# Streamed weight halves: three transfers of 640 columns in place of two of 960

## The chip, the cores and the metric

The kernel runs on one core of one Trainium2 chip. The metric is the device time of one execution in microseconds; the median of several runs is compared. A profiled execution, taken by the hardware profiler, gives the trace that the views below are read from.

## The reference

Four layers are applied in turn to x (2,048 positions of 640 columns), each as `x = x + layer(layernorm(x))`: layer A, layer B, layer A, layer B, with the same weights for both A and both B.

```python
# A: a recurrence over 64 segments of 32 positions, with 8 memory rows
for s in range(n_seg):
    h = concat([mem, xs])                  # 40 rows of 640
    q, k, v = h @ Wq, h @ Wk, h @ Wv       # 32 heads of 192 each
    p = softmax(mask(q @ k.T * scale))
    o = (p @ v) @ Wo
    mem, out = o[:8], o[8:]                # the memory of the next segment
# B: sliding dilated attention, window 8, dilation 2, 32 heads of 20
q, k, v = x @ wqkv
o = attention(q, k[pos - 2*w], v[pos - 2*w], w = 0..7) @ wo
```

Everything is bf16. The memory rows make the segments of layer A a strict sequence, so its weights (Wq, Wk, Wv, Wo, each 640 x 6,144) are needed again for every segment.

## The kernel before

**Steps.** `run` makes 67 steps (t = 0 to 66), written out in full. In step t, layer 1 works on segment t and layer 3 on segment t - 2, side by side as two lanes of 40 rows (80 columns of every matmul). Layers 2 and 4 (B) follow one step behind. The step's matmuls on TensorE are laid down in a fixed order by hand (`manual_schedule`): for each of eight groups of four heads ("quads", i = 0 to 7) the projections k, q, v (`proj`, matmuls at L264), the scores, the values, and with a lag of five quads the output projection (`a_o`, matmuls at L381). The matmuls of B are put between them. VectorE, ScalarE and GpSimd empty PSUM, take exponentials and normalise beside this.

**Weights.** Each quad of each of the four weights is cut into two halves. A half is a tile of 128 partitions by `HALF` = 1,920 bf16 columns (3,840 bytes in a partition, 480 KB). There are 64 halves. SBUF holds 41 of them for the whole run (`wres`); the other 23 are *streamed*: they are loaded anew in every step into a ring of four tiles (`wring`, all with the name w_ring), spread evenly over the step's TensorE work (`resident_halves`). For k, q and v the half's columns are five chunks of the contraction, 384 columns each, and the first matmuls go through all five chunks; for o they are three blocks of 640.

**Loads.** All weight loads are issued by SyncE's queue, in the order in which TensorE consumes the halves. `prefetch` is called by `used` whenever a half has been read for the last time, which frees a slot of the ring:

```python
t_ = self.wring.tile([P, HALF], BF16, name="w_ring")
self.ring_free -= 1
kind, i, h = key
piece = HALF if self.n_loaded < N_HALVES else PIECE
self.n_loaded += 1
for c0 in range(0, HALF, piece):
    self.nc.sync.dma_start(out=t_[:, c0:c0 + piece], in_=self.wsrc[kind][i, h, :, c0:c0 + piece])
```

The loads of the first pass, all 64 halves, are one transfer of 480 KB each. From then on a streamed half is loaded in pieces of `PIECE` columns. The line that issues them is L226. A load into a ring slot waits on SyncE until TensorE's last matmul on the slot's former half is done, and SyncE's queue is in order: what stands behind a waiting load waits too. The weight loads of TensorE wait for the piece that holds their columns, not for the whole half. B's weights are loaded once, in the second pass. ScalarE's queue carries the input segments and the results.

Of the kernel before, what the change touches and what calls it, by code (L numbers as in the profile page):

```python
# [38 lines left out]
BDIL = 2  # L39

HALF = 1920
PIECE = 960
N_HALVES = 64
N_RES = 41
RING = 4
# [33 lines left out]
class Kernel:  # L79
# [130 lines left out]
    def prefetch(self):  # L210

        while self.loads and (self.loads[0] in self.resident or self.loads[0][0] == "b" or self.ring_free):
# [9 lines left out]
# [3 lines that stand above are left out]
# [693 lines left out]
```

## Time and profile before

| | |
|---|---|
| runs | 3134.16, 3138.03, 3148.04 us; median 3138.03 |
| the profiled execution | 3135.55 us, of which the span is 3133.8 |
| granted TensorE clock, mean | 0.992 |
| busy: PE, DVE, ACT, POOL | 98%, 76%, 59%, 18% |
| DMA, mean over the span | 251 GB/s |
| transfers of streamed halves in pieces | 2,990 of 240 KB |
| median us from issue to landing of these | 3.8 to 4.1, by weight |

PE is TensorE, PEld its weight loads, DVE is VectorE, ACT is ScalarE, POOL is GpSimd, SP is SyncE and SPq its queue of instructions. Busy time leaves out the issuing of transfers. In the chain of waits that ended last, 95% of the span lies on PE. The names in a row read "out<-in"; L264 is line 264 of the kernel. "Landing" is the moment at which a transfer's completion has arrived from all of its DMA engines.

### The profile page before, as it was taken

To read this page: it belongs to the slowest core of one execution; us is meant where nothing else is said; L and a number is where in the kernel's file an instruction comes from. 1 tells how busy PE (TensorE), PEld (TensorE's weight loads), DVE (VectorE), ACT (ScalarE), POOL (GpSimd) and SP (SyncE) were. 2 spreads that over 40 slices of the span, in tenths; PEclk is the share of its full clock that TensorE was granted. 3 is DMA by queue.
4 is the path that set the end of the run, shared out by engine and by line. 5 is a ranking of instruction groups with operands and counts; after the bars stand their busy time and mean duration, and the time that the engine had idled before them with its cause. 6 is when DMAs were issued, how large, how long until landed. Compare 5 with 4: busy or idle time off the path is not lost.

```text
span 3133.8 us, 187134 instructions
## 1 busy us (share of the span) xinstructions
PE 3080.9 (98%) x83420; PEld 3031.6 (97%) x83420; DVE 2375.7 (76%) x6019; ACT 1851.2 (59%) x5613; POOL 555.5 (18%) x1012
## 2 busy tenths in 40 slices
PE   6899999999999999999999999999999999999998
PEld 4899999999999999999999999999999999999997
DVE  3677777777777777777777777777777777777776
ACT  2456656656656656656656656655655655655654
POOL 2112111111111111111111111111111121121121
PEclk7999999999999999999999999999999999999999
DMA  9877777877778778777877877777778878777776
GB/s 390 294 251 248 246 247 246 249 246 249 246 245 249 248 246 250 246 246 247 250 244 250 248 244 249 249 246 246 248 244 248 249 245 249 248 244 244 249 248 215
DMA packets 455705, 786.98 MB, mean 251 GB/s; under 512 B 58864, under 2 KB 445680, under 8 KB 454896
## 3 DMA queue, kind: packets, MB, share of 16 engines
q1 hardware_dynamic: 441216, 769.80, 77.7%
q8 instruction: 652, 10.68, 1.4%
q10 hardware_dynamic: 13680, 5.21, 0.7%
q14 instruction: 157, 1.29, 0.1%
HBM read 772.19 MB, written 2.62 MB: 247 GB/s over the span
## 4 chain that ended last, share of the span: by engine, by line
PE 95%; DMA 3%; DVE 1%; ACT 0%; issue 0%; SPq 0%; ACTq 0%; DVEq 0%
PE ps_acc L381 18%; PE ps_k L264 17%; PE ps_q L264 17%; PE ps_v L264 17%; PE ps_vt L318 5%; PE ps_o L351 5%; PE ps_s L330 2%; PE ps_s L331 2%; PE ps_bs L538 2%; PE ps_bv L495 2%; PE ps_by L594 2%; PE ps_bk L495 1%; PE ps_bq L495 1%; DMA w_q<-in_A_Wq_dram 1%; PE ps_vr L298 1%; PE ps_bo L561 1%
## 5 line engine op out<-in xcount | busy, mean ns | idle before, releaser
L355 ACT ACTIVATE R<-ps_o 64x160 f32<-64x160 f32 (+1 forms) x2112 | 622.2, 295 | 336.6 <-PE ps_o L351 120.0
L264 PEld LDWEIGHTS <-w_ring 128*128 128x128 bf16 x16530 | 679.2, 100 | 20.9 <-issue 4.5
L526 POOL TENSOR_TENSOR QX<-QB,hmask 128x448 bf16<-128x448 bf16 (+1 forms) x325 | 311.3, 966 | 1339.5 <-ACT QB L505 1029.6
L264 PE MATMUL ps_q<-hT,w_q 128*128 128x80 bf16 (+1 forms) x12870 | 540.8, 201 | 3.4 <-DMA w_q<-in_A_Wq_dram 3.4
L264 PEld LDWEIGHTS <-w_q 128*128 128x128 bf16 x12870 | 493.5, 100 | 4.5 <-DMA w_q<-in_A_Wq_dram 4.4
L381 PE MATMUL ps_acc<-OT,w_o 128*128 128x80 bf16 (+1 forms) x9900 | 458.5, 201 | 2.7 <-DMA w_o<-in_A_Wo_dram 2.1
L276 ACT CAST KF<-ps_k 128x320 bf16<-128x320 f32 (+1 forms) x528 | 218.9, 415 | 406.6 <-PE ps_k L264 398.4
L309 DVE CAST vT<-ps_v 128x480 bf16<-128x480 f32 (+1 forms) x504 | 329.0, 653 | 161.3 <-PE ps_v L264 143.0
L283 DVE CAST QT<-ps_q 128x480 bf16<-128x480 f32 (+1 forms) x528 | 337.2, 639 | 115.4 <-PE ps_q L264 112.4
L264 PE MATMUL ps_v<-hT,w_v 128*128 128x80 bf16 (+1 forms) x9480 | 422.9, 201 | 1.8 <-DMA w_v<-in_A_Wv_dram 1.4
L381 PEld LDWEIGHTS <-w_o 128*128 128x128 bf16 x9900 | 392.9, 100 | 3.7 <-DMA w_o<-in_A_Wo_dram 2.5
L264 PE MATMUL ps_k<-hT,w_ring 128*128 128x80 bf16 (+1 forms) x7920 | 374.8, 200 | 6.5 <-DMA w_ring<-in_A_Wk_dram 2.7
L264 PE MATMUL ps_k<-hT,w_k 128*128 128x80 bf16 (+1 forms) x7920 | 374.6, 201 | 2.9 <-DMA w_k<-in_A_Wk_dram 1.5
L264 PEld LDWEIGHTS <-w_v 128*128 128x128 bf16 x9480 | 371.3, 100 | 2.3 <-DMA w_v<-in_A_Wv_dram 1.7
L333 ACT ACTIVATE E<-ps_s 80x320 bf16<-80x320 f32 (+1 forms) x528 | 221.1, 419 | 248.2 <-PE ps_s L331 248.1
L365 DVE TENSOR_TENSOR OT<-ps_o,R 128x320 bf16<-128x320 f32 (+1 forms) x528 | 254.0, 481 | 139.2 <-ACT R L357 118.2
L264 PEld LDWEIGHTS <-w_k 128*128 128x128 bf16 x7920 | 321.2, 100 | 3.8 <-issue 2.0
L320 DVE COPY Vt<-ps_vt 80x768 bf16<-80x768 bf16 x504 | 279.1, 554 | 54.8 <-PE ps_vt L318 42.9
L381 PE MATMUL ps_acc<-OT,w_ring 128*128 128x80 bf16 (+1 forms) x5940 | 308.2, 201 | 2.3 <-DMA w_ring<-in_A_Wo_dram 1.7
L264 PE MATMUL ps_v<-hT,w_ring 128*128 128x80 bf16 (+1 forms) x5640 | 264.4, 202 | 0.7 <-DMA w_ring<-in_A_Wv_dram 0.7
L339 DVE TENSOR_TENSOR E<-E,maskA 80x320 bf16<-80x320 bf16 (+1 forms) x528 | 207.3, 393 | 63.5 <-ACT E L333 52.9
L357 ACT ACTIVATE R<-R 128x320 f32<-128x320 f32 (+1 forms) x528 | 243.9, 462 | 16.6
(142 smaller groups left out, 4930.1 us busy)
## 6 DMA issues: line engine op xcount, KB each, us to landing
w_ring<-in_A_Wk_dram SPq DMA_DIRECT2D x1040, 240.0 KB, 3.8
w_ring<-in_A_Wv_dram SPq DMA_DIRECT2D x780, 240.0 KB, 4.1
w_ring<-in_A_Wo_dram SPq DMA_DIRECT2D x780, 240.0 KB, 3.8
w_ring<-in_A_Wq_dram SPq DMA_DIRECT2D x390, 240.0 KB, 3.9
w_q<-in_A_Wq_dram SPq DMA_DIRECT2D x13, 480.0 KB, 8.7
w_v<-in_A_Wv_dram SPq DMA_DIRECT2D x10, 480.0 KB, 9.6
w_o<-in_A_Wo_dram SPq DMA_DIRECT2D x10, 480.0 KB, 9.6
w_ring<-in_A_Wk_dram SPq DMA_DIRECT2D x8, 480.0 KB, 7.5
```

Of the source, the lines that this page charges most:

```text
L264: nc.tensor.matmul(ps[:, NT * n + self.c0:NT * n + self.c1], lhsT=w[n // 3][:, c, P * (n % 3):P * (n % 3 + 1)], rhs=hT[:, NT * c + self.c0 ...
L276: nc.scalar.copy(out=kf, in_=pv[:, :, 0:3:2, :])
L283: self.nc.vector.tensor_copy(out=self.cols(qt[:]), in_=self.cols(ps[:, 0:6 * NT].rearrange("p (a n) -> p a n", a=6)))
L309: nc.vector.tensor_copy(out=self.cols(self.vT[:, 0:6 * NT].rearrange("p (a n) -> p a n", a=6)), in_=self.cols(ps[:, 0:6 * NT].rearrange("p ...
L320: nc.vector.tensor_copy(out=vt[0:NT, :].rearrange("p (a b c) -> p a b c", a=2, b=2)[:, :, :, 0:DH], in_=ps[0:NT].rearrange("p (a b) c -> p ...
L333: nc.scalar.activation(out=self.cols(e[0:NT]), in_=self.cols(sv[0:NT]), func=ACT.Exp, scale=float(DH) ** -0.5)
L339: nc.vector.tensor_tensor(out=self.cols(e[0:NT]), in0=self.cols(e[0:NT]), in1=self.cols(self.maskA[0:NT, :]).unsqueeze(1).to_broadcast([NT ...
L355: nc.scalar.activation(out=self.cols(r[r0:r0 + 64, :, j]), in_=self.cols(src), func=ACT.Ln)
L357: nc.scalar.activation(out=rf, in_=rf, func=ACT.Exp, scale=-1.0)
L365: nc.vector.tensor_tensor(out=oc[:, :, 0:3:2], in0=ov[:, :, 0:4:3], in1=r, op=ALU.mult)
L381: nc.tensor.matmul(self.cols(acc[:, k]), lhsT=w[m // 3][:, m % 3, P * c:P * (c + 1)], rhs=self.cols(ot[:, m]), start=(i == 0 and m == 0 an ...
L526: self.nc.gpsimd.tensor_tensor(out=qx[:, 0:nh, :], in0=self.qb[:, c, :].unsqueeze(1).to_broadcast([P, nh, NX]), in1=self.hmask[c][:].unsqu ...
```

## The change

```diff
 HALF = 1920
-PIECE = 960
+PIECE = 640
 N_HALVES = 64
```

A streamed half, from the second pass on, is loaded by three transfers of 640 columns (1,280 bytes in each partition, 160 KB) in place of two of 960 columns (1,920 bytes, 240 KB). The order of the loads, the ring, the matmuls and everything on the other engines stand as they were.

## The prediction

> **What bounds the kernel now.** I read the page first, for the engine at its limit; then the waits of TensorE in the steady part of the run, for what a faster transfer could win; then the SyncE queue, which issues the transfers that change.
>
> ```profile
> span 3133.8 us, 187134 instructions
> PE 3080.9 (98%) x83420; PEld 3031.6 (97%) x83420; DVE 2375.7 (76%) x6019; ACT 1851.2 (59%) x5613; POOL 555.5 (18%) x1012
> q1 hardware_dynamic: 441216, 769.80, 77.7%
> ```
>
> TensorE is busy in 98% of the span; the queue that carries the weights (q1) keeps the 16 DMA engines busy for 77.7% of it. The next lines are the windows view (span, then busy us of each engine with its count, granted clock, DMA share, GB/s): the first pass over the weights, the second, and the steady part.
>
> ```profile
> 0.00:83.00 83.00, 51.03 (x1023) 39.09 (x1024) 28.46 (x88) 19.92 (x77) 21.79 (x108) 0.79 1.00 390
> 83.00:132.50 49.50, 43.06 (x1126) 36.70 (x1123) 28.93 (x92) 22.22 (x85) 8.46 (x15) 0.93 0.90 305
> 200.00:3090.00 2890.00, 2883.71 (x78466) 2857.97 (x78463) 2239.85 (x5627) 1746.45 (x5252) 508.94 (x866) 1.00 0.80 247
> ```
>
> In 200 to 3090 us TensorE is idle for 6.3 us of 2,890. Of the waits over 150 ns there (engine, what it waited for: us in total, times, longest), one is for a transfer, of 0.5 us:
>
> ```profile
> PE ps_k L264 <- issue: 2.2, 5, 0.7
> PE ps_vr L298 <- ACT Kz L278: 1.0, 2, 0.5
> PE ps_acc L381 <- issue: 0.8, 2, 0.6
> PE ps_acc L381 <- DMA w_ring<-in_A_Wo_dram: 0.5, 1, 0.5
> ```
>
> So the change has almost nothing to win; the question is how much of the cover it uses up. The SyncE timeline (start, us, count) and two rows of the ring tile's view (count: shortest/median/longest ns of one issue; and us to landing) show that cover:
>
> ```profile
> 1500.26 0.81 SPq L226 DMA_DIRECT2D w_ring<-in_A_Wq_dram  x2
> 1505.61 0.81 SPq L226 DMA_DIRECT2D w_ring<-in_A_Wv_dram  x2
> 1513.83 1.16 SPq L226 DMA_DIRECT2D w_ring<-in_A_Wq_dram  x2
> 1506.79 0.60 PEld L264 LDWEIGHTS <-w_ring 128*128 128x128 bf16 x15
> L226 SPq DMA_DIRECT2D w_ring<-in_A_Wk_dram x1048: 327/430/1975, 1.2 to 3094.4; - x175
> DMA to landing us min/median/max: 2.5/3.9/9.7
> ```
>
> The half issued at 1500.26 and 1500.63 landed at 1503.24 and 1503.86 and is first read at 1506.8: about 3 us to spare. I matched all 1,380 streamed halves of steps 4 to 63 in this way (issue, landing of the last transfer, first weight load that reads it). The spare time of the last transfer is 0.06 us at least, 1.28 at the 5th percentile, 2.77 in the median. If every last transfer came later by d, the matmuls would miss this much in all: d=0.2 us, 0.2 us (3 halves late); 0.3, 0.6 (4); 0.75, 3.6 (12); 1.0, 8.2 (25); 1.25, 18.2 (63); 1.5, 40.7 (110); 2.0, 136 (293). That table prices everything below.
>
> **What is removed, added and moved.** 1,495 streamed halves (2,990 transfers of 240 KB) become 4,485 transfers of 160 KB; the first 64 halves stay whole.
>
> *Bytes.* These do not change; the rows of a packet shrink from 1,920 to 1,280 B. In the trace's packet records the median packet takes 79 ns at 1,920 B, 102 at 2,560 and 32 at 640: a line on which 1,280 B is 55. Each engine moves 8 packets and one completion of 9 ns per transfer, so a half costs 16 x 79 + 18 = 1.28 us now and 24 x 55 + 27 = 1.35 after: +0.06. The mean packet is longer (97 ns), a few per cent being held up; if that strikes per packet, 8 more packets at 18 ns add 0.14. On today's mean of 1.57 us per half that is +4% to +13%: the DMA share of 0.80 goes to between 0.83 and 0.91, still below full.
>
> *Issue.* The pair of issues is 0.37 + 0.43 us; the third adds 0.43 and a gap of 0.05. SyncE then needs 1.33 us per half, and halves come 2.04 us apart, so the queue does not saturate. For a half that starts on a free queue the third issue costs almost nothing: the second lands 3.15 us after the first issue at best now (0.37 + 2.78), and the third goes out at 0.85 and a transfer of 160 KB takes 2.47 - 0.19 = 2.28 at best: 3.13. I take d = 0.25 for such halves, nearer to the packet rows than to the bounds of 0.05 and 0.5.
>
> *Queue behind it.* 358 of the 1,380 halves (26%) are issued right behind another; SyncE is in order, so the extra 0.48 us is theirs too: d = 0.73. By their own spare times they miss 2.2 us. The rest (64% after the next step's 14%) miss 0.4 x 0.64 = 0.2.
>
> *Long issues.* Some issues take far longer than 0.43: after 200 us, 365 of 2,870, with 0.75 us extra in the mean (tenth 0.31, ninetieth 1.21). They fall on 24% of the second issues of an unbroken run and 14% of the third, rarely twice in a run. Before, no half had a third issue of its own: bounds none and 24%; I take 14%. Then d is 0.56, 1.0 or 1.46 for these halves; the table gives about 2, 8 and 40, a mean of 17, and 14% of it is 2.4. The 3.6% that stand behind such a half have d near 1.5: 41 x 0.036 = 1.5.
>
> *Waking.* These are about 19 waits, each with some 0.1 us to resume (bounds 0 and 0.23, the latter the time from the last matmul of a slot to SyncE's issue): 2. The third transfer's satisfied wait on a weight load costs nothing: matmuls that follow such a load stand 36 ns apart, as do the others.
>
> *First passes.* In 83 to 132.5 us the DMA share is 0.90 and the first shorter transfers run beside the last resident loads: 0 to 2 us, I take 1.
>
> The sum: 0.2 + 2.2 + 2.4 + 1.5 = 6.3 over 60 steps, 7 over all streamed passes, and with 2 and 1 it is **10 us**. The span becomes 3143.8. The profiled run took 3135.55 (1.75 beyond its span), 2.5 below the median of the three runs, so the median becomes 3138.0 + 10 = **3148**. With the low ends (d = 0.05, no long third issue) the loss is 2; with the high ends (d = 0.5, 24%) the same sum gives about 23, and 27 with pushes down the queue.
>
> A smaller gain stays possible: columns 0 to 639 land some 0.2 us earlier than 0 to 959 did. But the first columns are not the late ones (2 of 1,380 have under 1 us to spare), so it is worth at most the 0.5 us above.
>
> **Rivals.** *Slower by much: eight transfers in flight.* The transfers take eight completion semaphores in turn, and in the first step each issue waits for the transfer eight places earlier. This shows in the waits of SyncE (two rows of that view):
>
> ```profile
> SPq L226 <- DMA w_q<-in_A_Wq_dram: 7.6, 10, 0.9
> SPq L226 <- DMA w_o<-in_A_Wo_dram: 7.5, 9, 0.9
> ```
>
> With two per half, eight back is the ring slot's own old load, long landed. With three, the third transfer of a half waits for the first of the half two before it. Against it: 8 x 164 KB in 3.5 us is 374 GB/s, above the 247 needed, and at today's times only 36 of 1,380 would wait, 0.24 us each. It decides once a first transfer lands about 4.3 us after its issue (median now 3.7, 4.6 in one of ten), since the halves two apart are issued within 3.5 us in a quarter of cases. Then d is near 1.25 for all: 18, long issues at d = 2 add 0.14 x 136 = 19, waking 8: +45, that is **3183**, from +30 to +60. For it: SyncE stands still meanwhile, and every half behind it is late too.
> The Trainium skill, "DMA: Bandwidth & Descriptors" (Rules for kernel authors; Anatomy of one DMA), points this way: it wants 1 MiB and more per transfer, and gives, for transfers issued from GpSimd, some 2.0 us fixed plus bytes at 436 GB/s. By that formula a transfer would take 2.56 us before and 2.38 after; the trace's shortest, 2.5, agrees with the first, and nothing here yet shows the second. If none of the fixed part were hidden, 1,495 more transfers would add 2,990 us, an estimate that the overlap in the timeline excludes.
>
> *No change: all of it hidden.* If the third issue catches no long stall and the landing spread stays, the loss is 0 to 3 us: **3139**. For it: the median spare of 2.77 us. Against: the long issues are there on every place in a run.
>
> *Faster.* Only through 0.5 us of waits, or a run-to-run difference. That the edit does not act is excluded by the three slices of 640 in 1,920.
>
> **How the numbers follow.** A loss of 10 us (2 to 27): 0.52. The eight in flight: 0.28. Hidden: 0.17. Faster: 0.03. A difference of 0.5% is 15.7 us, about what a measurement of this kernel can tell from no change. Above it lie the upper quarter of the first case (0.13) and the second case: slower 0.41; faster 0.03; the same 0.56. The range runs from just below the median of before, for the hidden case, to the middle of the second case: 3136 to 3184. For the likeliest case alone it is 3140 to 3165.
>
> **What would show it.** Right: in 200 to 3090 us some 10 to 40 TensorE waits for w_ring transfers, 5 to 20 us in all, mostly on halves issued behind another; issues of 430 ns, x4485; the DMA share at 0.83 to 0.91; steps of TensorE otherwise as long as before. The eight-in-flight rival: SyncE waits for DMA w_ring by the hundred in the steady part, and a landing median well above 3.9. Hidden: as good as no TensorE wait for a transfer. I am wrong if the matmuls themselves slow down, if the DMA share reaches 0.95, or if the SyncE queue never empties.

## The result and the profile after

Three transfers are slower: the ratio of nine runs each is 1.0027, with a 95% interval of 1.0017 to 1.0036, which is +8.5 us (5.3 to 11.3). The medians are 3149.07 us against 3143.13, 5.9 us apart. The profiled runs lie further apart: spans of 3146.0 and 3133.8, since the profiled run of before (3135.55) was one of its fastest. Single runs of one kernel spread over some 16 us; e3 below shows part of why.

The page of the changed kernel, and its chain of waits by engine (the chain had 95% on PE and 3% on DMA before):

```profile
span 3146.0 us, 188628 instructions
q1 hardware_dynamic: 656496, 769.90, 79.9%
PE 92%; DMA 6%; SPq 1%; DVE 1%; ACT 0%; issue 0%; ACTq 0%; DVEq 0%
```

The bytes are the same and the weight queue's share has gone from 77.7% to 79.9%. What is new is that 3% more of the chain lies on transfers and 1% on SyncE's queue. The same windows as in the prediction:

```profile
83.00:132.50 49.50, 42.52 (x1087) 36.04 (x1088) 27.44 (x85) 21.58 (x83) 8.43 (x15) 0.93 0.91 292
200.00:3090.00 2890.00, 2880.38 (x78286) 2853.47 (x78284) 2236.14 (x5617) 1741.23 (x5240) 505.55 (x865) 1.00 0.82 247
```

In the second pass TensorE gets through fewer matmuls in the same 49.5 us (1,087 against 1,126). In the steady part its idle time grows only from 6.3 to 9.6 us. TensorE's waits there:

```profile
PE ps_acc L381 <- DMA w_ring<-in_A_Wo_dram: 5.4, 9, 1.0
PE ps_k L264 <- DMA w_ring<-in_A_Wk_dram: 1.7, 5, 0.9
PE ps_bk L495 <- issue: 0.6, 1, 0.6
```

Two things moved, in opposite directions. The waits for w_ring transfers rose from 0.5 us to 7.5. The "issue" waits, in which no semaphore keeps TensorE, fell from 4.0 us to 0.6.

The first k matmuls of the steps, matched one by one in the two traces, say where the 12.2 us of the two spans lie: the first pass +0.2; step 1 (the second pass) 49.3 to 50.7, +1.4; step 2 +0.7; steps 3 to 63 +4.5; step 64 41.9 to 43.2, +1.4; from the start of step 65 to the end 55.7 to 59.7, +4.0. This last stretch does the same work in both, 1,295 matmuls (first before, then after):

```profile
3078.10:3133.80 55.70, 46.98 (x1295) 40.70 (x1291) 33.65 (x107) 25.77 (x96) 5.14 (x6) 0.93 0.59 192
3086.20:3146.00 59.80, 49.56 (x1295) 41.62 (x1291) 33.54 (x108) 25.70 (x96) 5.27 (x6) 0.91 0.61 185
```

For steps 3 to 63 I compared each matmul's start with the usual one at the same place in the step (46.72 us for an undisturbed step in both kernels). Late transfers cost 0.3 us before and 8.6 after; lateness without any semaphore 5.1 before and 1.2 after; other engines 1.3 and 1.7.

SyncE's timeline points to the cause of the late transfers. First before, then after:

```profile
2001.46 0.80 SPq L226 DMA_DIRECT2D w_ring<-in_A_Wk_dram  x2
2003.62 0.80 SPq L226 DMA_DIRECT2D w_ring<-in_A_Wv_dram  x2
2005.69 2.81 SPq L226 DMA_DIRECT2D w_ring<-in_A_Wk_dram  x4
2008.89 0.80 SPq L226 DMA_DIRECT2D w_ring<-in_A_Wv_dram  x2
```

```profile
2000.47 5.32 SPq L226 DMA_DIRECT2D w_ring<-in_A_Wo_dram  x9
2007.31 1.28 SPq L226 DMA_DIRECT2D w_ring<-in_A_Wk_dram  x3
2008.69 1.32 SPq L226 DMA_DIRECT2D w_ring<-in_A_Wv_dram  x3
2010.66 2.36 SPq L226 DMA_DIRECT2D w_ring<-in_A_Wk_dram  x3
```

Before, the queue pauses after most halves, waiting for a slot. After, the pauses are fewer and shorter; nine issues in a row are three halves. In 200 to 3090 us one issue takes 0.52 us in the mean (0.43 in the median), so with the gaps a half takes 1.76 us of SyncE's 2.04, where it took 1.13. Of the 1,380 halves, 57% start right behind another (26% before). The last transfer's time to spare falls from 2.77 to 2.07 us in the median, and at the 5th percentile from 1.28 to 0.38. 31 halves come late (1 before): 30 of them stood behind another half, and 2 had a long issue (over 0.6 us) of their own. In steps 1, 64 and 65, outside this count, 20 of 69 halves come late (5 before), and 74%, 61% and 87% start right behind another (26%, 35% and 39% before).

### The profile page after: what moved, and what is told of

It reads as the page before. It is cut to its first block, busy times and chain, and to the rows that moved or that the text cites. A ratio compares the mean times of both kernels' runs of the same rounds, so it can differ in the third digit from the quotient of the medians.

```text
span 3146.0 us, 188628 instructions
## 1 busy us (share of the span) xinstructions
PE 3087.9 (98%) x83420; PEld 3034.7 (96%) x83420; DVE 2374.6 (75%) x6019; ACT 1848.3 (59%) x5613; POOL 553.7 (18%) x1012
## 3 DMA queue, kind: packets, MB, share of 16 engines
q1 hardware_dynamic: 656496, 769.90, 79.9%
q8 instruction: 652, 10.68, 1.5%
## 4 chain that ended last, share of the span: by engine, by line
PE 92%; DMA 6%; SPq 1%; DVE 1%; ACT 0%; issue 0%; ACTq 0%; DVEq 0%
PE ps_acc L381 17%; PE ps_k L264 17%; PE ps_q L264 17%; PE ps_v L264 16%; PE ps_vt L318 5%; PE ps_o L351 5%; PE ps_s L330 2%; PE ps_s L331 2%; PE ps_bs L538 2%; DMA w_ring<-in_A_Wo_dram 2%; PE ps_by L594 1%; DMA w_ring<-in_A_Wk_dram 1%; PE ps_bv L495 1%; PE ps_bk L495 1%; PE ps_bq L495 1%; SPq L226 1%
## 5 line engine op out<-in xcount | busy, mean ns | idle before, releaser
L264 PEld LDWEIGHTS <-w_ring 128*128 128x128 bf16 x16530 | 680.7, 100 | 26.7 <-DMA w_ring<-in_A_Wk_dram 10.4
L381 PEld LDWEIGHTS <-w_ring 128*128 128x128 bf16 x5940 | 249.7, 100 | 11.3 <-DMA w_ring<-in_A_Wo_dram 8.9
```

The costliest lines, as they stand in the source:

```text
L264: nc.tensor.matmul(ps[:, NT * n + self.c0:NT * n + self.c1], lhsT=w[n // 3][:, c, P * (n % 3):P * (n % 3 + 1)], rhs=hT[:, NT * c + self.c0 ...
L381: nc.tensor.matmul(self.cols(acc[:, k]), lhsT=w[m // 3][:, m % 3, P * c:P * (c + 1)], rhs=self.cols(ot[:, m]), start=(i == 0 and m == 0 an ...
```

## The experiments

Each kernel has 4 to 11 timed runs, beside 15 to 27 of the kernel before. "Late" and "instructions" are the two sums for steps 3 to 63 that were explained above, from the profiled run of each.

| kernel | ratio to before, 95% | late, us | instructions, us |
|---|---|---|---|
| before | 1 | 0.3 | 5.1 |
| 640 columns (the change) | 1.0027 (1.0017 to 1.0036) | 8.6 | 1.2 |
| e1: 960, 896, 64 | 1.0043 (1.0030 to 1.0056) | 5.4 | 8.4 |
| e2: 1,280, 640 | 1.0065 (1.0052 to 1.0078) | 1.4 | 28.1 |
| e3: empty instructions | 0.9998 (0.9988 to 1.0008) | 0 | 11.3 |
| e4: 1,920 | 1.0125 (1.0109 to 1.0141) | 0.2 | 43.4 |
| e5: four of 480 | 1.1455 (1.1438 to 1.1471) | 382 | under 1 of waits |
| e6: five slots, 960 | 1.0018 (1.0009 to 1.0026) | 1.7 | 16.1 |
| e7: five slots, 640 | 1.0015 (1.0006 to 1.0024) | 2.1 | 2.0 |
| e8: 640 but for the last steps | 1.0022 (1.0012 to 1.0032) | 10.2 | 3.3 |
| e9: 640 in steps 2 to 63 only | 0.9999 (0.9990 to 1.0008) | 7.9 | 1.5 |
| e10: 640 outside them only | 1.0022 (1.0013 to 1.0031) | 1.0 | 7.9 |
| e11: five slots, 640 in steps 2 to 63 | 0.9985 (0.9976 to 0.9994) | 2.4 | 4.5 |

**e1, a tiny third transfer.**

```diff
-PIECE = 960
+CUTS = (0, 960, 1856, 1920)
...
+            for c0, c1 in zip(cuts, cuts[1:]):
```

> Three transfers of 960, 896 and 64 columns: the issues of the changed kernel with nearly the rows of the kernel before. Theory (SyncE's in-order queue pays 0.48 us more for each half, and the halves behind it start late): as the changed kernel, +5 to +14 us, more than half of the halves issued right behind another, TensorE waits of 5 to 12 us for w_ring in 200 to 3090 us. Rival A (eight transfers in flight): the same loss, but with hundreds of SyncE waits for w_ring transfers. Rival B (shorter rows of 1,280 bytes load more slowly): no loss, 0 +- 3 us.

The number of issues makes transfers late, with the rows nearly as before: 53% of the halves behind another, 5.4 us late. Rival B, the shorter rows, falls for that part. Rival A is weakened only: SyncE waited 113 times, 37 us in all, for a ring transfer (27 times and 13 us in the changed kernel), though only 2 of the 16 late halves stood in a run of issues with such a wait. But the kernel is slower than the changed one at the point estimate, and the difference in the profiles stands in the other column: with a largest transfer of 960 the instruction waits stay.

**e2, an uneven pair.**

```diff
+CUTS = (0, 1280, 1920)
```

> Two transfers of 1,280 and 640 columns: the issues of the kernel before, a third of the bytes in rows of 1,280. Theory: 0 +- 3 us, about 26% of the halves behind another. Rival A: 0. Rival B: +2 to +5 us.

Every theory on record missed this: +0.65%, more than the change itself. The halves are not late (26% behind another, 2.75 us to spare in the median). TensorE's waits in 200 to 3090 us show what happened:

```profile
PE ps_k L264 <- issue: 4.8, 12, 0.6
PE ps_v L264 <- issue: 4.1, 11, 0.7
PE ps_q L264 <- issue: 2.3, 3, 1.4
```

These waits are for no semaphore. The page has a queue that carries instructions:

```profile
q8 instruction: 652, 10.68, 1.4%
```

In the trace's packet records it brings blocks of 16 KB, one every 4.7 us. The 10.68 MB are 64 bytes for each of the 166,840 matmuls and weight loads, and the 652 blocks are the same in every run, whatever SyncE issues: I take q8 for TensorE's program. The weight loads that end the 59 such waits of e2 start 1.28 to 1.59 us (5th to 95th percentile) after a block has been transferred, though blocks come only every 4.7 us: TensorE is waiting for its own instructions.

**e3, a loaded SyncE without transfers.**

```diff
+            if self.n_loaded > N_HALVES:
+                for _ in range(10):
+                    self.nc.sync.nop()
```

> The kernel before, with ten empty instructions on SyncE behind the two issues of each streamed half, which I expect to take 0.3 to 0.6 us together, and no further transfer. Theory: if they take about 0.48 us, as the changed kernel, +4 to +14 us, with the same lengthening of the time from a slot's release to the first issue (mean 0.36 to about 0.7 us). Rivals A and B: 0 +- 3 us, since neither the transfers in flight nor the rows change.

The empty instructions do not stand in the program that ran (187,134 instructions, as before), so this says nothing on SyncE's time. It is a second sample of the kernel before: the same time, but 11.3 us of instruction waits where the other profile has 5.1. The profiled run took 3143.07 us, 7.5 more than the other, and 6.2 of these are instruction waits.

**e4, one transfer.**

```diff
-PIECE = 960
+PIECE = 1920
```

> One transfer of 1,920 columns for each streamed half. Theory: SyncE's queue is emptier (under 20% of the halves behind another), but TensorE waited for a transfer only 0.5 us in the steady part before, so at most 2 us are won; the first columns land 0.6 us later and the last about as before: -3 to +2 us. Rival A: the same. Rival B: a gain of up to 3 us.

The emptiest queue (4% behind another, 2.96 us to spare) gives +1.25%, where -3 to +2 us was expected. Its steady window, and TensorE's waits in it:

```profile
200.00:3090.00 2890.00, 2858.32 (x77340) 2828.56 (x77338) 2212.35 (x5542) 1726.87 (x5169) 498.86 (x851) 1.00 0.77 243
```

```profile
PE ps_k L264 <- issue: 6.6, 12, 1.3
PE ps_q L264 <- issue: 6.5, 13, 1.1
```

TensorE is idle for 32 us of this window with a DMA share of 0.77, the lowest of all: so a busier set of DMA engines is not what makes the instructions late. By the largest transfer of a half, the "issue" waits of TensorE's weight loads in this window are 0.2 us at 480 columns (e5), 3.2 at 640 (the change), 8.0 at 960 (before), 25.7 at 1,280 (e2) and 39.9 at 1,920 (e4). Single profiles scatter: the other kernels of the table have about 4 to 7 us with 640 in the steady steps and 10 to 18 with 960. In e5 TensorE is idle for 221 us of the window, above all for late transfers, which may also give its program time to arrive. The rows of a transfer grow with its columns, so these runs do not separate the size of a transfer from the length of its rows.

**e5, four transfers.**

```diff
+PIECE = 480
```

> Four transfers of 480 columns. The runs so far say that two things move: TensorE's waits for late transfers (8.6 us in steps 3 to 63 with 640 columns, 0.3 with 960) and its waits for instructions, which end about 1.4 us after the landing of a 16 KB block of program (1.2 us with 640 columns, 5 to 11 with 960, 28 with the pair 1,280 and 640, 43 with 1,920). Theory (SyncE's in-order queue makes the late transfers): 1.8 us of issues for a half every 2.04 us nearly fill the queue, so over 80% of the halves start behind another and the waits for transfers grow to 40 to 150 us; instruction waits under 2 us; +30 to +140 us in all. Rival (eight transfers in flight, two halves): more, +100 us and above, with SyncE waits for w_ring transfers by the hundred, hundreds of us in total. Rival (only the size of the transfers counts): a gain of 0 to 5 us.

The direction was right, the size not: +14.6%, for the queue is not nearly full but overfull. SyncE's timeline and TensorE's waits:

```profile
1499.04 3.04 SPq L226 DMA_DIRECT2D w_ring<-in_A_Wv_dram  x4
1502.18 2.89 SPq L226 DMA_DIRECT2D w_ring<-in_A_Wk_dram  x4
1505.17 1.81 SPq L226 DMA_DIRECT2D w_ring<-in_A_Wq_dram  x4
```

```profile
PE ps_k L264 <- DMA w_ring<-in_A_Wk_dram: 92.1, 155, 2.3
PE ps_acc L381 <- DMA w_ring<-in_A_Wo_dram: 71.7, 104, 2.3
```

Four issues with their gaps take 2.34 us of SyncE; halves now come every 2.33 us. The rival with eight in flight had to show in SyncE's waits for transfers, and these are 4.8 us in 14 times, beside 382 us of late transfers. Issue time it is.

**e6 and e7, a fifth slot.**

```diff
-N_RES = 41
-RING = 4
+N_RES = 40
+RING = 5
```

(e6 is the kernel before with this edit, e7 the changed kernel with it.)

> The kernel before with five ring slots and 40 resident halves, so 24 streamed halves in each step. Theory: no transfer is late, the instruction waits stay (5 to 12 us in steps 3 to 63): 0 +- 4 us against before. Rivals: the same.

> Three transfers of 640 with five ring slots and 24 streamed halves. Theory: the fifth slot gives each half about 2 us more to spare, so the late transfers go (under 2 us of TensorE waits for w_ring in 200 to 3090 us) and the shorter instruction waits remain (about 1 us): -4 to -9 us against before, faster than both kernels. Rival (eight transfers in flight set the lateness): a fifth slot doesn't help, since the eighth transfer back is the same: the waits for transfers stay at 7 us or more, SyncE waits for w_ring transfers grow, +3 us or more.

e6 has no late transfers to speak of, as expected, but at +0.18% it lies above the 0 +- 4 us, with instruction waits of 16.1 us. In e7 the mechanism came out as expected: with 640 columns the fifth slot brings the late transfers from 8.6 to 2.1 us, though SyncE now waits 36 us in all (89 times) for the transfer eight places back; the rival that makes these waits the cause falls. The steady steps of e7 are as good as those of the best profile of before. But the total did not follow: 1.0015, no better than e6, where -4 to -9 us was expected. In e7 step 1 takes 54.3 us (47.7 in e6), step 64 takes 44.0 (41.3), and from step 65 on it is 58.5 (55.4).

**e8, the last steps spared.**

```diff
+PIECE3 = 640
...
+            piece = HALF if self.n_loaded < N_HALVES else (PIECE3 if N_HALVES <= self.n_loaded < N_HALVES + 23 * 63 else PIECE)
```

> Three transfers of 640 up to the loads of step 63, two of 960 in those of the last steps (64 and 65), in which one lane runs and TensorE has less work for each half. Theory: the 5 us that the profile of the changed kernel shows lost after step 63 come back: 4 to 6 us faster than the changed kernel, +1 to +5 us against before. Rival (these 5 us come from elsewhere, as from the spread of single runs): as the changed kernel, +6 to +11 us.

By the times this is inconclusive, 1.0022 against 1.0027 of the changed kernel, with wide intervals. In its profile the stretch from step 65 on is back at 55.2 us, but step 64 stays at 43.5 and step 1 takes 54.0.

**e9, e10 and e11, steady steps and edges.**

```diff
+            n_str = N_HALVES - N_RES
+            steady = N_HALVES + n_str <= self.n_loaded < N_HALVES + n_str * 63
+            piece = HALF if self.n_loaded < N_HALVES else 640 if steady else PIECE
```

(e10 has `not steady`; e11 is e9 with `N_RES = 40` and `RING = 5`.)

> Ring of four as before; 640 columns only for the loads of steps 2 to 63, 960 for those of step 1 and of the last steps. Theory, with three parts: late transfers in the steady steps +9, shorter instruction waits there -4 to -9, and the second pass (step 1) and the one-lane steps at the end, where three issues per half cost 4 to 9 us together, spared: -2 to +4 us against before. Rival (the loss sits in the steady steps alone): +6 to +10 us as the changed kernel.

> The complement: 640 columns only for the loads of step 1 and of the last steps (64 and 65), 960 for those of steps 2 to 63. Theory: +4 to +10 us against before, with the time between the first k matmuls of steps 1 and 2 at about 54 us in place of 48 to 50, and the stretch after the start of step 65 at 58 to 60 in place of 55.7. Rival (loss in the steady steps alone): 0 +- 3 us.

> Five ring slots and 40 resident halves, 640 columns for the loads of steps 2 to 63 and 960 for the others. Theory: no late transfers in the steady steps (under 2 us), instruction waits there of about 2 us in place of 5 to 16, and the edges as before: -4 to -9 us against before, and -8 to -13 against the changed kernel. Rival (the instruction waits in single profiles are chance and do not follow the transfer size): 0 to +6 us, as the kernel with five slots and 960 columns.

These say where the loss sits. 640 columns in the steady steps alone change nothing (0.9999), and 640 in the loads of step 1 and of the last two steps alone cost +0.22%, 7 us (4 to 10): nearly the whole loss of the change. Over all profiles with two or three transfers in equal parts, step 1 takes 46.6 to 50.5 us where its loads have 960 columns and 50.7 to 54.3 where they have 640; from step 65 on it is 55.2 to 56.3 and 56.9 to 59.7. Step 64 tells less: 43.5 us in e10 and 41.0 in e9, but also 43.5 in e8, whose loads there are those of e9. In e10 step 1 took 51.0 us and the last stretch 56.9, both below what I had expected. Which edge weighs more stays open: in the profile of the changed kernel it is the end, but e8 and e9 differ in the loads of step 1 alone, and their ratios by 0.23%, though the two were not run side by side. The steady steps of e9 hold both sides of the trade:

```profile
PE ps_acc L383 <- DMA w_ring<-in_A_Wo_dram: 2.4, 5, 0.8
PE ps_v L266 <- DMA w_ring<-in_A_Wv_dram: 1.1, 2, 0.8
PE ps_k L266 <- DMA w_ring<-in_A_Wk_dram: 0.9, 3, 0.4
PE ps_s L333 <- issue: 0.4, 1, 0.4
```

e11 has 640 columns in the steady steps, adds the slot that hides most of the late transfers, and leaves the edges alone. It beats both kernels: 0.9985 of before, 4.7 us less (1.9 to 7.5), with 3138.74 us in the median. The total is as expected; the late transfers (2.4 us) and the instruction waits (4.5, against 5.1 to 16.1 with 960 columns) are each somewhat above the 2 us expected. Its steady window and two of TensorE's waits in it:

```profile
200.00:3090.00 2890.00, 2883.98 (x78467) 2857.67 (x78465) 2239.35 (x5625) 1744.26 (x5253) 508.63 (x868) 1.00 0.85 258
```

```profile
PE ps_v L266 <- issue: 1.4, 3, 0.9
PE ps_k L266 <- DMA w_ring<-in_A_Wk_dram: 0.6, 2, 0.3
```

## Why the prediction was right, and where its terms were not

The forecast of +10 us met +8.5, but the total is right in part because errors cancelled. That the median of 3149.07 lies 1 us from the forecast 3148 is luck as well: the forecast started from 3138.0, the median of three runs, and nine runs have 3143.1. The signs named for the main case came: in 200 to 3090 us TensorE waited 15 times, 7.5 us in all, for ring transfers (10 to 40 times and 5 to 20 us were named).

*The queue behind a half* was the right mechanism: 30 of the 31 late halves stood behind another. Its term was mis-sized at its root. I took 1.33 us of SyncE per half from medians and kept the 26% of halves behind another. Long issues and gaps count too: 1.76 us were measured, and 57%. So the 6.3 us forecast for late transfers in the steady steps became 8.6. For a half on a free queue the time from the first issue to the last landing grew by 0.37 us in the median (4.38 to 4.75), where I took 0.25.

*Long issues of a half's own* (2.4 + 1.5 us of the sum) fall as a term: 2 of 31 late halves had one. They act by filling the queue: 30 of the 31 had one in the unbroken run of issues up to their own (72% of all halves had).

*Waking* was taken too high: the late weight loads start some 0.04 us after the landing, not 0.1.

*The first passes and the end* failed most. I allowed 1 us for the second pass and scaled the last steps with the others. They hold +7.7 us of the 12.2 in the profile, and e10 gives 7 by itself. In the second pass the DMA share is 0.91, and in the one-lane steps there are fewer matmuls to hide a load: step 64 lasted 41.9 us before, not 46.7, for the same 23 halves. The late halves there show it, 20 against 5. In the second pass B's weights, which stand in the same queue, come later too: TensorE's waits for them between 83 and 134 us went from 1.2 to 2.5 us.

*What could be won.* "Worth at most the 0.5 us above" was wrong. I had shown two "issue" rows of TensorE and read past them. Shorter transfers take 3.9 us off them in the two profiles; over all runs the kernels with 960 columns as the largest transfer of the steady steps have 5.1 to 16.1 us of them, those with 640 have 1.2 to 4.5. This gain cancelled the late transfers in the steady steps (e9).

*Bytes.* The median packet of 1,280 B takes 55 ns, as interpolated. From two to three transfers the hold-ups did not strike per packet: 11.5 ns of mean excess on 24 packets is 276 ns per half, against 288 before (e4 has 336 on 8 packets and e5 352 on 32), and the DMA share came to 0.82, under my 0.83 to 0.91.

*Rivals.* Eight in flight fell: landing medians are 3.7 to 4.0 us, SyncE waited 27 times, 13 us in all, for a ring transfer in the steady part, and 1 of the 31 late halves stood in a run of issues with such a wait. "Hidden" was refuted by the interval. The Trainium skill's formula for transfers issued from GpSimd ("DMA: Bandwidth & Descriptors", Anatomy of one DMA) gave 2.38 us for 160 KB; the shortest landing here is 2.2. The Trainium skill's preference for large transfers (the same page, Rules for kernel authors), given there for bandwidth, does not hold for the time of this kernel: e4, with the largest, is slower by 1.25%, and the measurement decides. The step from 640 to 480 columns goes its way.

## What to carry to other kernels

A transfer costs its issuing queue the mean of an issue with its gaps, not the median; multiply it by the transfers per period and look at how full the queue gets, since lateness grows long before 100%. When an engine is busy in 98% of the span, read its "issue" rows as well as its semaphore waits: they can be instructions that arrive late, and here the size of unrelated transfers moved them. Cost the first and last steps separately when they have less work per load.

## What the runs showed of the hardware that I had not expected

TensorE's waits for its own program grew with the length of the weight transfers, from 3.2 us at 640 columns to 39.9 at 1,920, with the same bytes in each step. The waits of e4 end 1.2 to 1.6 us after a 16 KB block has been transferred. That the block queues on its DMA engine behind the rows of a transfer in progress would fit; it was not tested.

The long issues of SyncE go with the same blocks. Of the 365 before, 346 end 1.25 to 2.5 us after the packet of such a block has started (median 1.35), and 512 of 548 after the change; of all issues, long or short, 39% and 35% end so. Which of the two holds up the other's start was not tried.
